# Cached attention on one core: V loaded head by head in K's key order, P normalized in blocks of 64

## The chip, the cores and the metric

The kernel runs on one core of one Trainium2 chip. The metric is the device time of one execution in microseconds (us). Before the change three runs gave 849.04, 850.43 and 854.05 us, median 850.43 us. The profile is of one further execution.

## The reference

Two independent blocks, A and B, of the same shapes are computed and laid side by side in the output. Each is attention over a cache, in bf16:

```python
B, Sq, D = 16, 64, 640            # batches, queries, model width
H, Sk, Dh = 32, 512, 128          # heads, cached keys, head width
q = (x @ wq).reshape(B, Sq, H, Dh).transpose(0, 2, 1, 3)
scores = einsum("bhqd,bhkd->bhqk", q, k_cache) * Dh ** -0.5
p = softmax(scores, axis=-1)
o = einsum("bhqk,bhkd->bhqd", p, v_cache)
out = o.transpose(0, 2, 1, 3).reshape(B, Sq, H * Dh) @ wo
```

Each of the four caches (K and V of A and B) has 16 x 32 x 512 x 128 elements of 2 bytes, 67.1 MB. They make up nearly all the 292 MB that the core reads.

## The kernel before

**Tiling.** The work is cut into 512 steps: a step is one head of two batches (a "batch pair"), 2 x 64 query rows on 128 partitions. Two steps are a macro-step, 256 in all; two macro-steps (four heads, G = 4) are a chunk. A pass is half of the heads (16) of one block over its 8 batch pairs; there are four passes.

**One macro-step m.** K of two heads and two batches comes by one load (LDK, L792, 512 KB) into the ring kn_ring. Partition p of a head holds the 8 consecutive keys 8p to 8p+7. TensorE transposes it in 32 pieces (KX, L586), so that column 64 t + p of the transposed K is key 8p + t; DVE copies that from PSUM to SBUF (KE, L593). Then per step: the scores (SM, L632), the negated row maximum on DVE (MX, L641), the exponential with row sum on ACT (EX, L647), the reciprocal on DVE (RC2, L653) and the normalization P times reciprocal on POOL (NM, L661), which writes pn_ring. TensorE transposes the normalized P in four pieces of 128 columns per step (TR2, L670); the transposed P is copied out of PSUM (TE on DVE, L680, or TA on ACT, L684), and TensorE multiplies it with V (PV2, L694). The results of a chunk leave PSUM on ACT (OE4, L701) and are multiplied with WO (OP2, L709, and OX, L719). The projection of Q (L603) and the transposes of x (L804, L813) run in between.

**Order of keys between P and V.** P's columns come in K's order, 64 t + p. V is loaded so that partition r holds the 4 consecutive keys 4r to 4r+3. NM closes the gap: it writes its columns in another order, so that piece tl of 128 columns has at place r the key 4r + tl:

```python
src = p_ring[:, g % NP, :].rearrange("q (th tl pp) -> q th tl pp", th=2, tl=4)
dst = pn_ring[:, g % NPN, :].rearrange("q (tl pp th) -> q th tl pp", tl=4, th=2)
```

Neighbours of the source land two elements apart in the destination.

**V.** One load per chunk and batch (LDV, L789, 512 KB, 256 in all) brings four heads of one batch into v_ring, which has 5 chunk slots (NVP). Each partition gets 4 x 1 KB. A slot is free for the load five chunks later once the second PV2 of its chunk has run.

**What sets the order.** Nothing is decided at run time. The order on TensorE, ACT, DVE and POOL comes from the templates PHASES: lists of (operation, offset in macro-steps, sub-index, due time in a period of 6.3 us), repeated for every chunk. Loads are sorted by a planned time and all issued on SP's queue, those of K, V, WQ, WO and x in one line; only the stores of the output are issued by ACT. The planner keeps a running time, which advances by DMA_US for each load (1.40 us for LDK, 1.44 for LDV), and makes each load wait for the TensorE operation that is planned just before it, at the latest BEFORE = 3.88 macro-steps ahead of its first use. LEAD and WLEAD are how far ahead loads are aimed for, STEP_US and START_US the planner's idea of TensorE's pace. Waits between engines are semaphores; a V slot has one semaphore of its own.

Of the kernel before, what the change touches and what calls it, by code (L numbers as in the profile page):

```python
# [15 lines left out]
class Cfg:  # L16
    G = 4
# [5 lines left out]
    LEAD = 5.37  # L23
    WLEAD = 5.48
    STEP_US = ((8, 3.68), (32, 27.17), (160, 3.12), (216, 3.1), (256, 3.43))
    DMA_US = dict(LDK=1.40, LDV=1.44, LDWQ=1.8, LDWO=1.8, LDX=0.45, LDXR=0.5)
    START_US = 210.96
    BEFORE = 3.88
# [17 lines left out]
         (("OE4", -4, 0, 0.38), ("QEZ", 0, 0, 0.43), ("QEZ", 0, 1, 1.68), ("OVP", -1, 0, 2.62), ("QEZ", 0, 2, 2.72),  # L46
          ("EX", 1, 0, 2.78), ("QEZ", 0, 3, 3.12), ("QEZ", 0, 4, 3.5), ("EX", 1, 1, 3.54), ("QEZ", 0, 5, 3.88),
          ("EX", 0, 1, 4.51), ("OXP", -13, 0, 4.63), ("QEJ", 4, 0, 4.64), ("TA2", -2, 0, 4.76), ("EX", 0, 0, 5.06),
          ("QEZ", 0, 7, 5.11), ("QEN", -6, 0, 5.12), ("QEZ", 0, 6, 5.49), ("ST", -45, 0, 6.19)),
         (("KE", 4, 0, 0.07), ("XIE", 2, 1, 0.91), ("MX", 0, 0, 0.95), ("MX", 0, 1, 0.96), ("RC2", -1, 0, 0.99),  # L50
          ("MX", 1, 0, 1.46), ("OXF", 47, 0, 2.01), ("MX", 1, 1, 2.78), ("OVF", -23, 0, 3.45), ("TE2", -1, 0, 3.61),
          ("XIE", 2, 2, 3.73), ("XIE", 2, 3, 3.96), ("KE", 3, 0, 4.55), ("XIE", 6, 0, 4.58), ("XIE", 0, 4, 4.84),
          ("XIE", -4, 6, 4.98), ("XIE", -2, 5, 5.43), ("RC2", 0, 0, 5.63), ("XIE", 0, 7, 6.21)),
# [6 lines left out]
         (("OE4", -4, 0, 0.38), ("QEZ", 0, 0, 1.23), ("OXP", -13, 0, 1.5), ("EX", 0, 1, 1.52), ("OVP", -17, 0, 1.59),  # L60
          ("EX", 0, 0, 1.89), ("XTE", 28, 0, 2.28), ("QEZ", 0, 1, 2.45), ("QEN", -6, 0, 2.53), ("ST", -35, 0, 3.16),
# [22 lines left out]
          ("QEN", -6, 0, 3.07), ("TA2", -2, 0, 3.72), ("OXP", -3, 0, 4.37), ("OVP", -3, 0, 4.78), ("EX", 1, 1, 5.06),  # L84
          ("XTE", 0, 0, 5.27)),
         (("KE", 3, 0, 0.07), ("RC2", -1, 0, 0.53), ("MX", 0, 0, 1.15), ("MX", 0, 1, 1.7), ("MX", 1, 0, 1.78),
          ("KE", 2, 0, 2.61), ("MX", 1, 1, 3.18), ("RC2", 0, 0, 3.78), ("OXF", -3, 0, 4.23), ("TE2", -1, 0, 4.74),
          ("OVF", -3, 0, 5.58)),
# [9 lines left out]
          ("OXF", -3, 0, 6.18)),  # L98
# [12 lines left out]
    )  # L111
    TRB = (2, 3)
    OXB = 4
    OXH = False
    KTB = (6, 6)
    NWU = 32

# [22 lines left out]
def build_plan(dims, cfg):  # L140
# [73 lines left out]
    def bank(i):  # L214
        return ("PB", i)
# [173 lines left out]
    def sem_key(op):  # L389
        if op.kind in ("LDK", "LDV", "LDXR"):  # L390
            return ("d_" + op.kind[2:].lower(), op.writes[0][1])
# [542 lines left out]
```

## Time and profile before

| what | value |
|---|---|
| median of three runs | 850.43 us (849.04 to 854.05) |
| profiled execution, time | 852.97 us |
| profiled execution, span from first to last instruction | 851.0 us |
| granted TensorE clock, mean | 0.998 |
| TensorE busy | 811.3 us (95%) |
| DVE busy | 727.9 us (86%) |
| ACT busy | 644.7 us (76%) |
| POOL busy | 417.1 us (49%) |
| read from HBM | 292.03 MB, 346 GB/s over the span with the 2.62 MB written |
| one V load (512 KB), issue to landing, median | 6.8 us in block A, 6.5 us in block B |
| one K load (512 KB), issue to landing, median | 6.5 us in block A, 6.3 us in block B |
| one normalization on POOL (L661) | 843 ns, 512 of them |

Busy times are summed over instructions of one engine, so shares of different engines overlap. "Issue to landing" runs from the DMA's issue on its queue to its completion. A packet in the profile's DMA rows is one contiguous piece that one DMA engine moves, or the small write with which an engine reports that its part of a transfer is complete. There are 16 DMA engines; "share of 16 engines" is the sum of all packets' times over 16 spans.

### The profile page before, as it was taken

Reading aid. Unit: us, or ns where it says so; the run is one execution under the profiler, and the core shown is the slowest. Engines: PE = TensorE matmul, PEld = TensorE weight load, DVE = VectorE, ACT = ScalarE, POOL = GpSimd, SP = SyncE. Lnnn points to the kernel's source line nnn. Section 1 sums busy time; section 2 is a strip of 40 time slices with the busy share of each in tenths; the row PEclk is TensorE's granted clock in tenths of the full one; section 3 lists DMA queues with packets and bytes.
Section 4 is the critical chain, followed back from the end, with each engine's and each line's share of the span. In section 5 each row is a group of like instructions: output and inputs, shape, how many; then the busy total and the mean of one; then the engine's idle time right before and its main releaser. Section 6 shows DMA issues by size and latency. Waiting matters only on the chain.

```text
span 851.0 us, 38366 instructions
## 1 busy us (share of the span) xinstructions
PE 811.3 (95%) x17025; PEld 566.4 (67%) x17156; DVE 727.9 (86%) x1192; ACT 644.7 (76%) x1466; POOL 417.1 (49%) x518
## 2 busy tenths in 40 slices
PE   8999999999999999999999998999999999999996
PEld 5566676666666666666666666666666666666664
DVE  4688888888888898888899887988888989989994
ACT  2678877777777787777877877787887877778886
POOL 0355455454544554454554545455455455455553
PEclk9999999999999999999999999999999999999999
DMA  9999999999999999999999999999999999999992
GB/s 306 360 354 349 369 354 352 348 338 362 354 352 353 369 369 363 359 360 367 364 362 367 364 360 349 321 362 362 360 360 363 366 369 365 366 339 352 370 321 89
DMA packets 228438, 297.14 MB, mean 349 GB/s; under 512 B 9136, under 2 KB 162736, under 8 KB 228272
## 3 DMA queue, kind: packets, MB, share of 16 engines
q1 hardware_dynamic: 225968, 292.06, 100.3%
q8 instruction: 134, 2.20, 1.1%
q10 hardware_dynamic: 2304, 2.62, 0.9%
q14 instruction: 32, 0.26, 0.1%
HBM read 292.03 MB, written 2.62 MB: 346 GB/s over the span
## 4 chain that ended last, share of the span: by engine, by line
PE 89%; issue 3%; ACT 3%; DMA 2%; DVE 2%; SPq 0%; ACTq 0%
PE ps L586 17%; PE ps L694 15%; PE ps L603 15%; PE ps L632 14%; PE ps L670 13%; PE ps L709 12%; PE ps L719 3%; ACT p_ring L647 2%; DMA v_ring<-in_A_v_cache_dram 1%; DVE negmax L641 1%; ACT pT_ring L684 1%; DMA wq_sb<-in_A_wq_dram 1%; DVE ktp_ring L593 1%; PE ps L804 0%; PE ps L813 0%
## 5 line engine op out<-in xcount | busy, mean ns | idle before, releaser
L661 POOL TENSOR_SCALAR pn_ring<-p_ring,recip 128x512 bf16<-128x512 bf16 x512 | 416.4, 843 | 425.1 <-DVE recip L653 379.0
L647 ACT ACTIVATE p_ring<-ps,negmax 128x512 bf16<-128x512 f32 x512 | 349.0, 688 | 74.0 <-DVE negmax L641 68.5
L593 DVE COPY ktp_ring<-ps 128x2048 bf16<-128x2048 bf16 x256 | 312.1, 1219 | 56.3 <-PE ps L586 56.2
L641 DVE TENSOR_REDUCE negmax<-ps 128x1 f32<-128x512 f32 x512 | 328.3, 683 | 16.2 <-PE ps L632 8.5
L586 PEld LDWEIGHTS ps<-ident,kn_ring 64*128 64x128 bf16 x8192 | 136.8, 95 | 107.9 <-issue 96.4
L586 PE MATMUL ps<-ident,kn_ring 64*128 64x64 bf16 x8192 | 169.2, 191 | 3.3 <-issue 1.4
L603 PE MATMUL ps<-xT_sb,wq_sb 128*128 128x512 bf16 (+2 forms) x543 | 133.4, 372 | 19.0 <-issue 18.1
L670 PEld LDWEIGHTS ps<-ident,pn_ring 128*128 128x128 bf16 x2048 | 125.4, 98 | 38.8 <-ACT p_ring L647 7.2
L694 PE MATMUL ps<-pT_ring,v_ring 128*128 128x64 bf16 x4096 | 143.5, 194 | 2.8 <-issue 1.9
L701 ACT ACTIVATE oT_ring<-ps 128x512 bf16<-128x512 f32 x128 | 76.4, 597 | 91.7 <-PE ps L694 91.7
L684 ACT ACTIVATE pT_ring<-ps 128x1024 bf16<-128x1024 bf16 (+1 forms) x144 | 140.9, 987 | 3.0 <-DVE pT_ring L680 2.2
L670 PE MATMUL ps<-ident,pn_ring 128*128 128x128 bf16 x2048 | 138.9, 219 | 3.4 <-issue 1.6
L709 PE MATMUL ps<-wo_sb,oT_ring 128*128 128x512 bf16 x498 | 135.3, 379 | 4.0 <-issue 1.9
L632 PE MATMUL ps<-ktp_ring,qc_ring 128*64 128x512 bf16 x1024 | 135.5, 385 | 0.7 <-issue 0.7
L694 PEld LDWEIGHTS ps<-pT_ring,v_ring 128*128 128x128 bf16 x4096 | 128.2, 98 | 9.6 <-issue 2.4
L647 ACT ACTIVATION_READ_ACCUMULATOR p_ring<-ps,negmax 128x1 f32 x512 | 104.8, 205 | 0.0
L680 DVE COPY pT_ring<-ps 128x1024 bf16<-128x1024 bf16 (+1 forms) x128 | 82.5, 644 | 14.6 <-PE ps L670 14.1
L619 ACT ACTIVATE qc_ring<-ps 128x512 bf16<-128x512 f32 (+1 forms) x129 | 76.8, 596 | 21.5 <-PE ps L603 21.4
L603 PEld LDWEIGHTS ps<-xT_sb,wq_sb 128*128 128x128 bf16 x660 | 53.8, 98 | 54.0 <-issue 1.1
L632 PEld LDWEIGHTS ps<-ktp_ring,qc_ring 128*64 128x64 bf16 x1024 | 47.2, 109 | 34.1 <-issue 1.3
L709 PEld LDWEIGHTS ps<-wo_sb,oT_ring 128*128 128x128 bf16 x512 | 42.7, 98 | 25.0 <-ACT pT_ring L684 2.1
L653 DVE RECIPROCAL recip<-rowsum 128x2 f32<-128x2 f32 x256 | 39.8, 155 | 4.4 <-ACT p_ring L647 4.4
(21 smaller groups left out, 127.2 us busy)
## 6 DMA issues: line engine op xcount, KB each, us to landing
kn_ring<-in_A_k_cache_dram SPq DMA_DIRECT2D x128, 512.0 KB, 6.5
v_ring<-in_A_v_cache_dram SPq DMA_DIRECT2D x128, 512.0 KB, 6.8
kn_ring<-in_B_k_cache_dram SPq DMA_DIRECT2D x128, 512.0 KB, 6.3
v_ring<-in_B_v_cache_dram SPq DMA_DIRECT2D x128, 512.0 KB, 6.5
wq_sb<-in_A_wq_dram SPq DMA_DIRECT2D x8, 640.0 KB, 7.1
wo_sb<-in_A_wo_dram SPq DMA_DIRECT2D x8, 640.0 KB, 7.2
wq_sb<-in_B_wq_dram SPq DMA_DIRECT2D x8, 640.0 KB, 6.8
wo_sb<-in_B_wo_dram SPq DMA_DIRECT2D x8, 640.0 KB, 6.6
```

The source lines that it names most:

```text
L586: last = e.transpose(kt_ps[hs][:, 64 * t:64 * t + 64], kn_ring[r, m % NKB, t // 8, t % 8 * DH:(t % 8 + 1) * DH], ident[r, r])
L593: ins = e.tensor_copy(ktp_ring[:, ktslot(op.idx)], ps[:, b:b + 2, :].rearrange("p b s -> p (b s)").bitcast(BF16))
L603: last = e.matmul(dst[:, col:col + n], wq_sb[:, qslot(hh // G), kt, (hh % G) * DH:(hh % G + 1) * DH], xT_sb[:, kt, lo * 128:hi * 128], sta ...
L632: ins = e.matmul(s_bank(g)[64 * j:64 * j + 64, :], q[:, 64 * j:64 * j + 64], kt[:, sub, j], start=True, stop=True, tile_position=(0, 64 * j))
L641: ins = e.reduce_max(negmax[:, r:r + 1], s_bank(g), axis=AX.X, negate=True)
L647: ins = e.activation(p_ring[:, g % NP, :], s_bank(g), ACTF.Exp, bias=negmax[:, r:r + 1], scale=1.0, accum_out=rowsum[:, r:r + 1])
L661: ins = e.tensor_scalar(dst, src, recip[:, r:r + 1], 1.0, ALU.mult, ALU.mult)
L670: ins = e.transpose(pt_flat(m)[:, (4 * sub + t) * 128:(4 * sub + t + 1) * 128], pn_ring[:, g % NPN, t * 128:(t + 1) * 128], ident[:, :])
L680: ins = e.tensor_copy(*pt_copy(op.idx, op.aux))
L684: ins = e.activation(*pt_copy(op.idx, op.aux), ACTF.Copy)
L694: ins = e.matmul(qo_ps[:, col:col + 64], v_ring[:, m // 2 % NVP, j, 2 * (m % 2) + sub, t * DH:(t + 1) * DH], pT_ring[:, m % NT, sub, t, 64 ...
L709: ins = e.matmul(out_ps, oT_ring[:, m // 2 % NO, 2 * (m % 2) + sub, :], wo_sb[:, wslot(ps_, hh // G), hh % G, 0:N0], start=(hh == 0), stop ...
```

## The change

V is loaded by one transfer per head and batch (128 KB, 1,024 in all) instead of one per four heads and batch. Within a head, partition th x 64 + p now holds the four keys 8p + 4 th to 8p + 4 th + 3, which is the numbering of K's rows. NM therefore leaves the 64 elements that belong to one (th, tl) together and only exchanges the order of these blocks. A PV2 waits for the four V transfers of its own two heads (one semaphore for each half of a V slot), and the slot's halves are freed and reloaded one by one. The planner's numbers and the templates PHASES are others: the kinds of operation in them are the same, at other due times and with some other offsets. The numbers of instructions of TensorE, ACT and DVE are unchanged.

```diff
-    LEAD = 5.37
-    WLEAD = 5.48
-    STEP_US = ((8, 3.68), (32, 27.17), (160, 3.12), (216, 3.1), (256, 3.43))
-    DMA_US = dict(LDK=1.40, LDV=1.44, LDWQ=1.8, LDWO=1.8, LDX=0.45, LDXR=0.5)
-    START_US = 210.96
-    BEFORE = 3.88
+    LEAD = 5.29
+    WLEAD = 5.77
+    STEP_US = ((8, 2.69), (32, 25.43), (160, 3.11), (216, 3.06), (256, 2.73))
+    DMA_US = dict(LDK=1.40, LDV=0.36, LDWQ=1.8, LDWO=1.8, LDX=0.45, LDXR=0.5)
+    START_US = 154.11
+    BEFORE = 3.97
...
     PHASES = (
...
         (112,
-         (("SM", 0, 0, 0.0), ("SM", 0, 1, 0.21), ("SM", 1, 0, 0.43), ("SM", 1, 1, 0.64), ("KX", 2, 0, 0.79),
-          ("OP2", -4, 0, 2.67), ("TR2", -2, 0, 2.98), ("OP2", -3, 0, 3.28), ("TR2", -1, 0, 3.46),
-          ("OX", -3, 0, 4.35), ("KX", 5, 0, 4.38), ("PV2", -2, 0, 5.77), ("PV2", -1, 0, 6.05)),
+         (("SM", 0, 0, 0.0), ("SM", 0, 1, 0.21), ("SM", 1, 0, 0.43), ("SM", 1, 1, 0.64), ("KX", 2, 0, 1.97),
+          ("OP2", -4, 0, 2.31), ("OP2", -3, 0, 3.17), ("TR2", -2, 0, 3.25), ("TR2", -1, 0, 3.28),
+          ("OX", -3, 0, 3.62), ("KX", 5, 0, 4.24), ("PV2", -2, 0, 4.74), ("PV2", -1, 0, 5.05)),
...
         if kind == "PV2":
-            return mk("pe", "PV2", m, [("pT", m % cfg.NT, 0), ("pT", m % cfg.NT, 1), ("v", k % cfg.NVP, 0), ("v", k % cfg.NVP, 1)], [bank(1)], ts)
+            return mk("pe", "PV2", m, [("pT", m % cfg.NT, i) for i in range(2)] + [("v", k % cfg.NVP, j, i) for j in range(2) for i in (g0 % G, g1 % G)], [bank(1)], ts)
...
-        add([("PV2", 2 * (k - cfg.NVP) + 1, 0)] if k >= cfg.NVP else [], ("PV2", 2 * k, 0), cfg.LEAD - j, 2, "LDV", m,
-            [("v", k % cfg.NVP, j)], m)
+        for i in range(G):
+            add([("PV2", 2 * (k - cfg.NVP) + i // 2, 0)] if k >= cfg.NVP else [], ("PV2", 2 * k + i // 2, 0), cfg.LEAD - j + i // 2, 2, "LDV", m,
+                [("v", k % cfg.NVP, j, i)], (m, i))
...
     def sem_key(op):
-        if op.kind in ("LDK", "LDV", "LDXR"):
+        if op.kind == "LDV":
+            return ("d_v", op.writes[0][1], op.aux[1] // 2)
+        if op.kind in ("LDK", "LDXR"):
             return ("d_" + op.kind[2:].lower(), op.writes[0][1])
...
         def em_NM(e, op):
-            src = p_ring[:, g % NP, :].rearrange("q (th tl pp) -> q th tl pp", th=2, tl=4)
-            dst = pn_ring[:, g % NPN, :].rearrange("q (tl pp th) -> q th tl pp", tl=4, th=2)
+            src = p_ring[:, g % NP, :].rearrange("q (th tl p) -> q th tl p", th=2, tl=4)
+            dst = pn_ring[:, g % NPN, :].rearrange("q (tl th p) -> q th tl p", tl=4, th=2)
...
-            if op.kind == "LDV":
-                h0 -= h0 % G
-                src = blocks[blk][2][2 * bp + m % 2, h0:h0 + G].rearrange("g (p t) d -> p g (t d)", p=128)
-                ins = e.dma_start(v_ring[:, m // 2 % NVP, m % 2], src)
...
+        def em_LDV(e, op):
+            m, i = op.aux
+            blk, bp, grp, ps_, hh0 = step_info(2 * m)
+            h = (ps_ % NHALF) * HH + hh0 - hh0 % G + i
+            src = blocks[blk][2][2 * bp + m % 2, h].rearrange("(p th t) d -> th p (t d)", th=2, t=4)
+            ins = e.dma_start(v_ring[:, m // 2 % NVP, m % 2, i], src)
+            return ins, ins
```

More of the change, by code (lines that the diff above doesn't have):

```diff
@@ L39 @@
         (0,
[6 rows of a table removed]
[L46 to L53, printed above, removed]
[6 rows of a table removed]
-         (("OE4", -4, 0, 0.38), ("QEZ", 0, 0, 1.23), ("OXP", -13, 0, 1.5), ("EX", 0, 1, 1.52), ("OVP", -17, 0, 1.59),
-          ("EX", 0, 0, 1.89), ("XTE", 28, 0, 2.28), ("QEZ", 0, 1, 2.45), ("QEN", -6, 0, 2.53), ("ST", -35, 0, 3.16),
[22 rows of a table removed]
[L84 to L88, printed above, removed]
[9 rows of a table removed]
-          ("OXF", -3, 0, 6.18)),
[12 rows of a table removed]
[6 rows of a table added]
@@ new lines @@
+         (("OVP", -15, 0, 0.19), ("OE4", -4, 0, 0.33), ("QEZ", 0, 0, 0.65), ("EX", 1, 0, 0.8), ("QEJ", 4, 0, 0.89),
+          ("QEZ", 0, 1, 1.6), ("QEZ", 0, 2, 2.06), ("OXP", -7, 0, 2.92), ("QEZ", 0, 3, 2.97), ("QEN", -6, 0, 3.31),
[4 rows of a table added]
+          ("OVF", -21, 0, 4.26), ("KE", 3, 0, 4.83), ("TE2", -1, 0, 4.83), ("XIE", 2, 2, 5.0), ("XIE", -2, 5, 5.21),
+          ("RC2", 0, 0, 5.23), ("XIE", -4, 6, 5.99), ("XIE", 2, 3, 6.01), ("XIE", 0, 7, 6.05)),
[7 rows of a table added]
+          ("EX", 0, 0, 2.38), ("QEZ", 0, 1, 3.21), ("QEN", -6, 0, 3.44), ("EX", 1, 0, 3.54), ("QEZ", 0, 2, 3.65),
+          ("TA2", -2, 0, 4.23), ("XTE", 30, 0, 4.73), ("QEZ", 0, 3, 4.84), ("OVP", -11, 0, 5.73), ("EX", 1, 1, 6.07)),
[10 rows of a table added]
+          ("XTE", -12, 0, 5.73)),
[10 rows of a table added]
+          ("OXP", -3, 0, 6.18)),
+         (("KE", 3, 0, 0.32), ("RC2", -1, 0, 0.52), ("MX", 0, 0, 1.32), ("MX", 0, 1, 1.76), ("MX", 1, 0, 1.8),
+          ("KE", 2, 0, 3.1), ("RC2", 0, 0, 4.68), ("TE2", -1, 0, 4.99), ("MX", 1, 1, 5.12), ("OVF", -3, 0, 5.13),
+          ("OXF", -3, 0, 5.79)),
[9 rows of a table added]
+          ("OVF", -3, 0, 5.7)),
[11 rows of a table added]
@@ L780, in em_LDX, with em_LDK @@
             return ins, ins
-        def em_LDKV(e, op):
+        def em_LDK(e, op):
             m = op.aux
@@ L785, in em_LDKV @@
             h0 = (ps_ % NHALF) * HH + hh0
-            if op.kind == "LDV":
-                h0 -= h0 % G
-                src = blocks[blk][2][2 * bp + m % 2, h0:h0 + G].rearrange("g (p t) d -> p g (t d)", p=128)
-                ins = e.dma_start(v_ring[:, m // 2 % NVP, m % 2], src)
-            else:
-                src = blocks[blk][1][2 * bp:2 * bp + 2, h0:h0 + 2].rearrange("j hs (p t) d -> (hs p) j (t d)", t=8)
-                ins = e.dma_start(kn_ring[:, m % NKB], src)
+            src = blocks[blk][1][2 * bp:2 * bp + 2, h0:h0 + 2].rearrange("j hs (p t) d -> (hs p) j (t d)", t=8)
+            ins = e.dma_start(kn_ring[:, m % NKB], src)
+            return ins, ins
[5 more added lines that the diff above has]
+            ins = e.dma_start(v_ring[:, m // 2 % NVP, m % 2, i], src)
             return ins, ins
@@ L839, in mha_kernel @@
                         OVP=em_OVP, OXP=em_OXP, OVF=em_OVF, OXF=em_OXF, ST=em_ST, INIT1=em_INIT1, INIT2=em_INIT2,
-                        LDWQ=em_LDWQ, LDWO=em_LDWO, LDX=em_LDX, LDXR=em_LDXR, XT=em_XT, XTE=em_XTE, XI=em_XI, XIE=em_XIE, WU=em_WU, LDK=em_LDKV, LDV=em_LDKV)
+                        LDWQ=em_LDWQ, LDWO=em_LDWO, LDX=em_LDX, LDXR=em_LDXR, XT=em_XT, XTE=em_XTE, XI=em_XI, XIE=em_XIE, WU=em_WU, LDK=em_LDK, LDV=em_LDV)
         def full(s, v):
```

96 rows, old and new, of the table PHASES are left out of this document.

## The prediction, made before the changed kernel ran

> **What bounds the kernel now.** I read the page's DMA parts first, because loads are what the change rewrites, then the waits of TensorE and of the SP queue, then the view of the V tile. Engines, DMA load and packets, from the page:
>
> ```profile
> PE 811.3 (95%) x17025; PEld 566.4 (67%) x17156; DVE 727.9 (86%) x1192; ACT 644.7 (76%) x1466; POOL 417.1 (49%) x518
> ...
> DMA  9999999999999999999999999999999999999992
> GB/s 306 360 354 349 369 354 352 348 338 362 354 352 353 369 369 363 359 360 367 364 362 367 364 360 349 321 362 362 360 360 363 366 369 365 366 339 352 370 321 89
> DMA packets 228438, 297.14 MB, mean 349 GB/s; under 512 B 9136, under 2 KB 162736, under 8 KB 228272
> ...
> q1 hardware_dynamic: 225968, 292.06, 100.3%
> q10 hardware_dynamic: 2304, 2.62, 0.9%
> ```
>
> TensorE is busy 95% of the span and the 16 DMA engines are busy in every slice but the last: two limits lie on top of each other. Of TensorE's own waits, the loads cause hardly any, while the SP queue, which issues every load, waits for TensorE again and again (columns: us in total, times, longest):
>
> ```profile
> PE ps L586 <- DMA v_ring<-in_A_v_cache_dram: 0.7, 1, 0.7
> ```
>
> ```profile
> SPq L792 <- PE ps L632: 103.6, 74, 2.9
> SPq L792 <- PE ps L709: 78.5, 73, 2.6
> ```
>
> So the loads arrive in time and are paced by TensorE, with little to spare: a load path that is somewhat slower has no idle engine to take it up. The V tile's view gives issue cost (min/median/max ns) and flight time:
>
> ```profile
> L789 SPq DMA_DIRECT2D v_ring<-in_A_v_cache_dram x128: 367/368/3549, 15.8 to 432.6; - x128
> L789 SPq DMA_DIRECT2D v_ring<-in_B_v_cache_dram x128: 367/368/1122, 436.3 to 834.9; - x128
> DMA to landing us min/median/max: 3.7/6.7/11.7
> ```
>
> Two more readings I need. First, the price of a packet on its DMA engine. In the trace's packet records 1,024-byte packets most often take 46 ns (mean 49.4), 2,048-byte ones 84 ns (mean 91.2), 1,280-byte ones 55 ns, and 4-byte completion packets 9 ns. Pricing all packets at these usual values fills 16 engines to 0.998 at most in any 21 us stretch and to 0.974 in the median one, so the usual values are one engine's service times, one packet after the other, and not overlapped latencies. Second, over how many engines a transfer is cut. There are 555 loads and 16 stores, 571 transfers; 571 x 16 = 9,136, exactly the packets under 512 B. So each transfer ends with one completion packet on every one of 16 engines. All 571 have access patterns that open with a count of 128 on both the HBM and the SBUF side.
>
> **The V load: how many engines.** Before, V's source is p g (t d): 128 x 4 x 512 elements. After, it is th p (t d): 2 x 64 x 512. The two outer counts can't be fused into 128, since th steps 1 KB and p steps 2 KB; the destination is still 128 partitions of one row. No transfer of before opens with anything but 128, so the number of engines a V load will use is not shown. The bounds are 16 (all 571 rows) and 2, if a transfer is dealt out along the outermost count of both sides: 2 and 128 have only 2 and 1 as common divisors. I take 2. The nearest rows agree with dealing along the outermost count and don't show any dealing inside it; the partition count alone, which stays 128, would give 16 and is the case against me.
>
> [...]
>
> **The sum with two engines, the same two each time.** V is 2 blocks x 16 x 32 x 512 x 128 x 2 bytes = 134.2 MB, 131,072 packets of 1 KB, unchanged in size and number. On two engines that is 65,536 each. Engine-time on either of them:
> - V: 65,536 x 46 ns = 3,015 us.
> - K stays on 16: 65,536 / 16 = 4,096 x 84 ns = 344 us.
> - WQ 10,240 / 16 x 46 ns = 29 us; WO and x 10,240 / 16 x 55 ns = 35 us; stores 7 us; completions (1,024 + 315) x 9 ns = 12 us; instruction fetch (1.1% of 851) 9 us.
> Together 3,451 us. Nothing hides it: per macro-step (one of 256) the two engines need 4 heads x 64 x 46 ns + 16 x 84 ns = 13.1 us, where TensorE's share now is 811.3 / 256 = 3.2 us. Loads are issued some four macro-steps ahead (BEFORE), some 50 us of work for the two engines, so they don't run dry, and K loads, which share the ring of those two engines, finish only behind V packets. V begins 16 us into the span and the last V load is issued 16 us before its end; about 13 us of the K, WQ and x work runs before V starts, and the end after the last V landing is 10 us: +13 us. Span about 3,465 us. The usual price of 46 ns is met by 66% of V-size packets while all 16 engines compete; with HBM traffic down to a quarter, I allow 0.4% over it: span 3,478, and the profiled execution's time stands 2.0 us above its span (852.97 against 851.0), so 3,480 us. The median of the runs is 850.43, 2.5 below the profiled one, which is nothing at this size.
>
> Bounds: at the shortest packets of the records (44 and 81 ns) V is 2,884 and K 332 us, the sum 3,308 and the time about 3,320. At the mean prices under today's contention (49.4 and 91.2 ns, others as above) V is 3,237, K 374, the sum 3,703 and the time about 3,720. A check from the page alone: 292.06 MB in 100.3% of 16 x 851 us is 21.4 GB/s per engine; 67.1 MB of V and 9.9 MB of the rest at that rate take 3,600 us, and at the best slice (370 / 16 = 23.1 GB/s) 3,330 us.
>
> **The other parts.** *Issues.* V goes from 256 to 1,024 transfers on SP's queue: +768. The nearest row is 0.367 us per issue whatever the size; for the unequal patterns take 0.367 to 1 us. A macro-step then has five issues, 1.8 to 5 us, hidden under 13.1 us; behind each V issue stand the K, WQ, WO and x loads of the same queue, and they are late only by what the two engines already impose. If the transfers kept 16 engines, that cover is gone: 1,323 SP issues x 0.367 = 486 us of 851, and the queue becomes the limit at 851 / 1,323 = 0.64 us each. *Completions.* With 16 engines 768 x 16 = 12,288 more packets, x 9 ns / 16 = 6.9 us; with two, fewer than now. *P in blocks of 64.* POOL's 512 normalizations (L661) take 843 ns for 512 elements with the written elements two apart; afterwards they run through blocks of 64. Not shown; bounds 0 gain to 843 ns gained, and on the other side double. POOL is busy 49%, 3.4 us (four of them) of a 6.3 us period of two macro-steps, so even double its time fits in a period of 26 us: nothing. *Ring freed by halves.* Each V load now waits only for the PV2 that reads its half chunk, up to one macro-step (3.2 us) earlier. With two engines the ring isn't short, nothing. *Order and pace.* The templates for TensorE, ACT, DVE and POOL are permuted and SP's planned times shifted; the instruction counts of TensorE, ACT and DVE are the same. TensorE is unoccupied for 851.0 - 811.3 = 39.7 us now, so the permutation is worth between -40 and, taken alike, +40 us where TensorE is the limit, and nothing where it waits for V.
>
> **The rivals.** *Sixteen engines after all, slower by completions (chance 0.06).* The partition count decides, or the pattern is re-cut. The engines are 97.4% filled by the usual prices, so 6.9 us more of packets go almost wholly to the end, 858 us (with the permutation unknown, 845 to 890). For it: the SBUF side is 128 as ever. Against it: the source can't be cut in 16 along its outermost count.
> *Sixteen engines, faster (0.04).* Finer V loads and earlier-freed halves even out the 0.974 filling: the 2.6% missing is 22 us, less 6.9 us for completions, so 837 us. It decides if completion packets lie in gaps rather than between data packets. Against it: the SP queue waits for TensorE and not for V slots.
> *Sixteen engines, SP the limit (0.01).* At 1 us an issue, 1,323 us. Against: every load row, 160 to 640 KB, has a median of 0.34 to 0.53 us.
> *Two engines, but another pair each time (0.02).* One V load then lasts 64 x 46 ns = 2.9 us instead of 1.5, inside the 6.7 us flight and the lead of four macro-steps; total engine work is unchanged, so about 851 us.
>
> **How the numbers follow.** Two engines, always the same: 0.87, because all 571 transfers are dealt out evenly where both sides open with 128 and nothing in the trace suggests that a count further in can be dealt out instead; time 3,480 us, own range 3,320 to 3,720. The range is this case's own, since the others together hold 0.13 and leaving them out is within 2 in 10. A measurement of this kernel tells apart about 0.5%. Faster by more than that: 0.04, the second rival. Within 0.5%: 0.03, the rotating pair and a part of the first rival. Slower: 0.87 + 0.05 + 0.01 = 0.93.
>
> **What would show it.** Right: packets under 512 B at 299 x 16 + 16 x 16 + 1,024 x 2 = 7,088 (with 16 engines 21,424); GB/s near 85 in all slices; the DMA row at 2 or 3 tenths with q1 near 25% of 16 engines; TensorE at some 23% and waiting above all for V; V's flight time in tens of us, because transfers queue on two engines. POOL's 512 normalizations near 0.8 us, whatever they are, would not matter. Wrong: 21,424 small packets and a time near 850; or 7,088 small packets with the DMA row still at 9 and a time near 850, which would mean that the pairs rotate; or two engines at a packet price clearly away from 46 ns, which would shift the time in proportion of 3,015 us.

## The result and the profile after

The changed kernel takes 3,268.61 us (median of 4 runs, 3,268.25 to 3,269.02) against 849.73 us (848.61 to 854.05) for the kernel before beside it: a ratio of 3.843, 95% interval 3.829 to 3.857. The direction and the mechanism are those of the prediction; the time is 6% under its 3,480 us and below its range, which began at 3,320.

The same rows of the page as for the kernel before, now of the changed kernel:

```profile
span 3266.9 us, 39264 instructions
...
PE 1126.0 (34%) x17156; PEld 737.7 (23%) x17156; DVE 740.0 (23%) x1192; ACT 667.6 (20%) x1466; POOL 349.7 (11%) x518
...
DMA  5222222222232222222222222222223222222221
GB/s 160 97 82 87 83 93 83 94 89 95 96 100 89 86 91 90 96 86 93 97 98 96 88 86 83 95 89 87 89 90 100 98 87 85 84 84 93 84 84 51
DMA packets 226396, 297.18 MB, mean 91 GB/s; under 512 B 7088, under 2 KB 160688, under 8 KB 226224
...
q1 hardware_dynamic: 223920, 292.06, 26.9%
```

The bytes and the number of V packets are the same, the mean fill of the 16 DMA engines fell from 9 tenths to 2, and the packets under 512 B are 7,088: 299 x 16 + 16 x 16 + 1,024 x 2. Each V load has left two completion packets, so each ran on two engines. A mean of 2 tenths does not mean that the DMA side has room: two engines of sixteen that never rest, and fourteen that carry only their part of K, give such a mean. The packet records bear this out. Packets of V's size start from 15.0 to 3,258.1 us of the span, and between 16 and 3,258 us two or more packets are in flight for all but 11 us, exactly two for 2,065 us. Pairs of engines that changed from load to load would have more V packets in flight at once. The records carry no engine's number, so they don't say which two.

What TensorE waits for (us in total, times, longest):

```profile
PE ps L695 <- DMA v_ring<-in_A_v_cache_dram: 1039.0, 62, 19.4
...
PE ps L695 <- DMA v_ring<-in_B_v_cache_dram: 1001.0, 64, 22.1
```

2,040 us of waiting stand ahead of PV2 (L695), in 126 waits for 128 chunks. The chain that ended last, by engine and by line, shows a trap:

```profile
SPq 58%; DMA 27%; PE 13%; issue 1%; DVE 0%; ACT 0%
SPq L797 44%; DMA v_ring<-in_A_v_cache_dram 14%; SPq L788 13%; DMA v_ring<-in_B_v_cache_dram 12%; PE ps L695 4%; PE ps L633 3%; PE ps L604 2%; PE ps L587 2%; PE ps L710 1%; PE ps L671 1%; DMA kn_ring<-in_A_k_cache_dram 1%; SPq L774 1%; DMA kn_ring<-in_B_k_cache_dram 0%; SPq L766 0%; SPq L802 0%
```

```profile
L797 SPq DMA_DIRECT2D v_ring<-in_A_v_cache_dram x512: 538/2808/4332, 15.1 to 1640.7; - x171
L797 SPq DMA_DIRECT2D v_ring<-in_B_v_cache_dram x512: 583/2658/4019, 1643.6 to 3248.0; - x171
```

The chain puts most on SP's queue, and a V issue lasts 2.7 us in the median. 1,024 of these would fill 2,800 us, so "SP has become the limit" reads as well from this page as "two engines are the limit". The minimum of 0.54 us speaks for back-pressure: SP can issue a V load in 0.54 us, and by my reading the issue is held up while the two engines still have work in line; no record shows how much they have. So do the issues of K, whose pattern did not change, with a median of 0.37 us before (L792) and 2.59 us after (L788):

```profile
L792 SPq DMA_DIRECT2D kn_ring<-in_A_k_cache_dram x128: 367/368/3161, 0.8 to 411.1; - x128
```

```profile
L788 SPq DMA_DIRECT2D kn_ring<-in_A_k_cache_dram x128: 368/2592/3357, 1.7 to 1560.3; - x128
```

The experiments decide it.

### The profile page after: what moved, and what is told of

Its sections match the earlier page's. It is cut to its first block, busy times and chain, and to the rows that moved or that the text cites. A ratio compares the mean times of both kernels' runs of the same rounds, so it can differ in the third digit from the quotient of the medians.

```text
span 3266.9 us, 39264 instructions
## 1 busy us (share of the span) xinstructions
PE 1126.0 (34%) x17156; PEld 737.7 (23%) x17156; DVE 740.0 (23%) x1192; ACT 667.6 (20%) x1466; POOL 349.7 (11%) x518
## 2 busy tenths in 40 slices
DMA packets 226396, 297.18 MB, mean 91 GB/s; under 512 B 7088, under 2 KB 160688, under 8 KB 226224
## 3 DMA queue, kind: packets, MB, share of 16 engines
q1 hardware_dynamic: 223920, 292.06, 26.9%
## 4 chain that ended last, share of the span: by engine, by line
SPq 58%; DMA 27%; PE 13%; issue 1%; DVE 0%; ACT 0%
SPq L797 44%; DMA v_ring<-in_A_v_cache_dram 14%; SPq L788 13%; DMA v_ring<-in_B_v_cache_dram 12%; PE ps L695 4%; PE ps L633 3%; PE ps L604 2%; PE ps L587 2%; PE ps L710 1%; PE ps L671 1%; DMA kn_ring<-in_A_k_cache_dram 1%; SPq L774 1%; DMA kn_ring<-in_B_k_cache_dram 0%; SPq L766 0%; SPq L802 0%
## 5 line engine op out<-in xcount | busy, mean ns | idle before, releaser
L695 PE MATMUL ps<-pT_ring,v_ring 128*128 128x64 bf16 x4096 | 242.4, 241 | 2040.0 <-DMA v_ring<-in_A_v_cache_dram 1039.0
L695 PEld LDWEIGHTS ps<-pT_ring,v_ring 128*128 128x128 bf16 x4096 | 222.1, 130 | 2055.5 <-DMA v_ring<-in_A_v_cache_dram 1046.3
L662 POOL TENSOR_SCALAR pn_ring<-p_ring,recip 128x512 bf16<-128x512 bf16 x512 | 349.0, 695 | 2873.7 <-PE ps L671 2314.6
L633 PE MATMUL ps<-ktp_ring,qc_ring 128*64 128x512 bf16 x1024 | 246.6, 619 | 46.9 <-DMA kn_ring<-in_B_k_cache_dram 46.9
L587 PE MATMUL ps<-ident,kn_ring 64*128 64x64 bf16 x8192 | 198.5, 206 | 13.1 <-DMA v_ring<-in_A_v_cache_dram 9.4
L587 PEld LDWEIGHTS ps<-ident,kn_ring 64*128 64x128 bf16 x8192 | 164.9, 105 | 137.2 <-issue 118.6
L710 PE MATMUL ps<-wo_sb,oT_ring 128*128 128x512 bf16 x512 | 180.6, 438 | 7.4 <-DMA kn_ring<-in_B_k_cache_dram 5.0
L604 PE MATMUL ps<-xT_sb,wq_sb 128*128 128x512 bf16 (+2 forms) x660 | 166.1, 387 | 0.4 <-ACT qc_ring L620 0.2
L671 PEld LDWEIGHTS ps<-ident,pn_ring 128*128 128x128 bf16 x2048 | 136.1, 102 | 43.5 <-issue 6.9
L633 PEld LDWEIGHTS ps<-ktp_ring,qc_ring 128*64 128x64 bf16 x1024 | 70.3, 157 | 132.7 <-issue 62.7
L604 PEld LDWEIGHTS ps<-xT_sb,wq_sb 128*128 128x128 bf16 x660 | 66.5, 105 | 87.5 <-issue 28.6
```

The costliest lines, as they stand in the source:

```text
L587: last = e.transpose(kt_ps[hs][:, 64 * t:64 * t + 64], kn_ring[r, m % NKB, t // 8, t % 8 * DH:(t % 8 + 1) * DH], ident[r, r])
L604: last = e.matmul(dst[:, col:col + n], wq_sb[:, qslot(hh // G), kt, (hh % G) * DH:(hh % G + 1) * DH], xT_sb[:, kt, lo * 128:hi * 128], sta ...
L633: ins = e.matmul(s_bank(g)[64 * j:64 * j + 64, :], q[:, 64 * j:64 * j + 64], kt[:, sub, j], start=True, stop=True, tile_position=(0, 64 * j))
L662: ins = e.tensor_scalar(dst, src, recip[:, r:r + 1], 1.0, ALU.mult, ALU.mult)
L671: ins = e.transpose(pt_flat(m)[:, (4 * sub + t) * 128:(4 * sub + t + 1) * 128], pn_ring[:, g % NPN, t * 128:(t + 1) * 128], ident[:, :])
L695: ins = e.matmul(qo_ps[:, col:col + 64], v_ring[:, m // 2 % NVP, j, 2 * (m % 2) + sub, t * DH:(t + 1) * DH], pT_ring[:, m % NT, sub, t, 64 ...
```

## The experiments

Theory A goes on from the completions so far (16 engines for 128 and 128, 2 for 2 and 128): a load runs on as many engines as the largest common divisor of the outer counts of its two patterns, up to the 16 that there are, and equal loads on the same ones. Its price comes from the changed kernel's packet records: where only V packets run, an engine starts a new one every 42 or 43 ns (381 ns for nine in a row; 42.35 ns in the mean), although each record lasts 46 ns. With two engines at work, the next start but one is the next on the same engine: in stretches of V-size packets alone it comes 42 or 43 ns later in 96,999 of 108,050 cases, and 46 ns later in 86. 2 KB packets start about every 80.3 ns (80 in unbroken rows) and last 84. The load of one of the two engines is then 65,536 x 42.35 ns = 2,775 us of V and 417 us of K and the rest, 3,192 us of the span of 3,267; 75 us are left for the ends and for contention. Rival B: SP's issues are the limit. Rival C: the price is the full 46 ns, as predicted, and something else saved time.

**Other outer counts.** Four variants of the changed kernel: V's source opens with 4, 8 or 16 (v_outer4, v_outer8, v_outer16), or the key order is undone with 128 rows and the old normalization (v_rows128).

```diff
v_outer4 (u=8 and u=16 in the other two):
-            src = blocks[blk][2][2 * bp + m % 2, h].rearrange("(p th t) d -> th p (t d)", th=2, t=4)
+            src = blocks[blk][2][2 * bp + m % 2, h].rearrange("(p u t) d -> u p (t d)", u=4, t=4)
v_rows128:
-            src = p_ring[:, g % NP, :].rearrange("q (th tl p) -> q th tl p", th=2, tl=4)
-            dst = pn_ring[:, g % NPN, :].rearrange("q (tl th p) -> q th tl p", tl=4, th=2)
+            src = p_ring[:, g % NP, :].rearrange("q (th tl pp) -> q th tl pp", th=2, tl=4)
+            dst = pn_ring[:, g % NPN, :].rearrange("q (tl pp th) -> q th tl pp", tl=4, th=2)
...
-            src = blocks[blk][2][2 * bp + m % 2, h].rearrange("(p th t) d -> th p (t d)", th=2, t=4)
+            src = blocks[blk][2][2 * bp + m % 2, h].rearrange("(p t) d -> p (t d)", t=4)
```

> V's source opens with 4 x 32 instead of 2 x 64 (partition u x 32 + p holds keys 16p + 4u to 16p + 4u + 3), all else as in the changed kernel; P is not reordered to fit, so V's rows stand beside other keys' P, with the same work. [...] Theory B (SP's issues of an unequal pattern are the limit, 2.6 us each as the changed kernel's row has them): 1,024 such issues as in the changed kernel, so 3,270 us again. Theory C (the packet price is the full 46 ns and something else saved time in the changed kernel): the step from 2 to 4 engines saves 1,507 us, so 1,760 us.

> V's source opens with 8 x 16, all else as in the changed kernel; P is not reordered to fit, with the same work. Theory A: an engine's load is 16,384 x 42.35 ns = 694 us of V and 417 us of the rest, 1,111 us, with ends and contention 1,130 to 1,210 us; 299 x 16 + 256 + 1,024 x 8 = 13,232 packets under 512 B. Theory B (SP issues): 3,270 us. Theory C (46 ns): 2 to 8 engines saves 2,261 us, 1,007 us.

> V's source opens with 16 x 8, so its outer count still differs from the destination's 128; all else as in the changed kernel; P is not reordered to fit, with the same work. Theory A: the largest common divisor is 16, the load of an engine is 347 + 417 = 764 us, less than TensorE's 811, so the time falls back to the kernel before: 840 to 890 us, with 299 x 16 + 256 + 1,024 x 16 = 21,424 packets under 512 B. Theory A' (only a pattern that opens with 128 on both sides is spread over all engines): well over 1,000 us. Theory B (SP issues, 2.6 us for an unequal pattern): 3,270 us; by the shortest issue of the changed kernel, 0.538 us, 1,024 x 0.54 + 299 x 0.37 = 661 us on SP, which does not limit. POOL's normalization: 695 ns if the blocks of 64 make it short, 843 ns if it was short only because the other engines idled.

> The key order is undone: V's source is 128 rows of 1 KB again and P is normalized in the old interleaved order; per-head loads, halves of a slot, planner numbers and templates stay those of the changed kernel. Theory A: 16 engines, 840 to 890 us; what is left against the kernel before is the price of per-head loads (6.9 us of completions if the engines' queues were the limit) and of the other order. Theory B: SP's issue at 0.37 us, 486 us on SP: 850 us too, so B is told apart by v_outer16 and not here. POOL's normalization: 843 ns.

Measured: 1,938.0 us with 4 and 1,361.6 us with 8 (one run each), 1,151.8 us with 16 (1.353 times before, interval 1.348 to 1.357), 854.5 us with 128 rows (1.0044, 1.0012 to 1.0077). The packet rows of the first three, in this order, one page each:

```profile
DMA packets 228444, 297.19 MB, mean 154 GB/s; under 512 B 9136, under 2 KB 162736, under 8 KB 228272
```

```profile
DMA packets 232540, 297.21 MB, mean 219 GB/s; under 512 B 13232, under 2 KB 166832, under 8 KB 232368
```

```profile
DMA  9999999999999999999999999999999999999994
...
DMA packets 240732, 297.24 MB, mean 258 GB/s; under 512 B 21424, under 2 KB 175024, under 8 KB 240560
...
q1 hardware_dynamic: 238256, 292.11, 103.1%
```

The completion packets are 9,136, 13,232 and 21,424 to the unit, which is 299 x 16 + 256 and 1,024 x 4, x 8 and x 16: 4, 8 and 16 engines per V load, as A has it. With 4, the records again have four or more packets in flight for all but 9 us from 16 us on to the last V packet. Rival B falls: the number of issues is the same in all of these and the time goes from 3,269 to 1,152 us. The median V issue goes from 2.7 us over 1.3 and 0.9 to 0.60 us at 16 engines:

```profile
L797 SPq DMA_DIRECT2D v_ring<-in_A_v_cache_dram x512: 536/600/4382, 14.7 to 586.8; - x171
```

The 2.7 us are about what the two engines need for one V load, 64 x 42.35 ns = 2.71 us. Rival C, which forecast 1,760 and 1,007 us with 4 and 8, falls too.

But the times miss A's as well, the more the more engines there are: 1,938 against A's sum for 4, 32,768 x 42.35 ns = 1,388 us of V and 417 us of the rest, 1,805 in all before ends and contention, 1,362 against 1,111, with ends and contention at most 1,210, and 1,152 against at most 890. The time with 16 fits A', but its reason does not: all 16 engines took part. With 16 engines A forecast TensorE as the limit again, and the DMA engines are full instead, at 258 GB/s. The packet records became longer: those of V's size last 47.2 ns in the mean on two engines, 49.7 on 4, 55.4 on 8 and 69.1 on 16, against 48.8 in v_rows128, where 16 engines move the same bytes. So a second thing depends on the outer count.

**What makes packets long.** Theory P: the side toward SBUF does it, where engines that are dealt runs of neighbouring partitions would collide; this is a guess, and no record names an engine or a partition. Theory H: the 16 KB steps of v_outer16 in HBM are slow. v_blocks8 keeps the 16 x 8 pattern and makes the HBM pieces contiguous; v_stride4k keeps 128 rows and spreads them in HBM; v_halves opens with 64 on both sides.

```diff
v_blocks8 and v_stride4k, from the changed kernel (the two last lines are one each):
-            h = (ps_ % NHALF) * HH + hh0 - hh0 % G + i
-            src = blocks[blk][2][2 * bp + m % 2, h].rearrange("(p th t) d -> th p (t d)", th=2, t=4)
+            h0 = (ps_ % NHALF) * HH + hh0 - hh0 % G
+            src = blocks[blk][2][2 * bp + m % 2, h0:h0 + G].rearrange("h k d -> (h k) d").rearrange("(u i p t) d -> i u p (t d)", i=4, p=8, t=4)[i]
+            src = blocks[blk][2][2 * bp + m % 2, h0:h0 + G].rearrange("h k d -> (h k) d").rearrange("(p i t) d -> i p (t d)", i=4, t=4)[i]
v_halves, from the kernel before, for th in (0, 1), with the changed kernel's normalization and LDV=0.72:
...
-                src = blocks[blk][2][2 * bp + m % 2, h0:h0 + G].rearrange("g (p t) d -> p g (t d)", p=128)
-                ins = e.dma_start(v_ring[:, m // 2 % NVP, m % 2], src)
+                src = blocks[blk][2][2 * bp + m % 2, h0:h0 + G].rearrange("g (p th t) d -> th p g (t d)", th=2, t=4)[th]
+                ins = e.dma_start(v_ring[64 * th:64 * th + 64, m // 2 % NVP, m % 2], src)
```

> Like v_outer16, V's source opens with 16 x 8 against 128 partitions, but the 8 rows of one outer index now lie together in HBM (8 KB in one piece, pieces 32 KB apart) where v_outer16 steps 16 KB between them; the four loads of a chunk and batch divide its 512 KB among themselves, so V's rows stand beside other heads' and keys' P, with the same work. Theory P (a load that is dealt out in runs of neighbouring partitions makes its engines collide on the SBUF side): packets as long as in v_outer16 (mean 69 ns), 1,120 to 1,180 us. Theory H (v_outer16 was slow because its engines step through HBM in 16 KB strides): packets near 49 ns again, 845 to 890 us.

> V's source opens with 128 as before, but its rows of 1 KB are 4 KB apart; per-head loads, P in blocks of 64, planner and templates as in the changed kernel; V's rows stand beside other heads' and keys' P, with the same work. Theory P: all 16 engines in the usual dealing, 845 to 870 us. Theory H: long packets, over 950 us. POOL under full load: 692 to 695 ns if the blocks make the normalization short, about 841 ns if the idling of others did.

> The kernel before with the change's key order, P in blocks of 64, and each V load split in two: 64 partitions by 4 heads, 256 KB, source and destination both open with 64, so that 16 engines take part; 512 V loads. Planner numbers of before, LDV 0.72. The result is the reference's. Theory A alone: 16 engines, 845 to 870 us. [...] POOL: 692 to 695 ns.

Measured: v_blocks8 1,160.3 us (1.359, 1.350 to 1.368), v_stride4k 856.6 us (1.0074, 1.0053 to 1.0095), v_halves between 1,248.7 and 1,282.9 us in four runs, above the 870 us of A and above what P allowed: even V packets at twice 42.35 ns, 8,192 x 84.7 = 694 us on an engine, make only 1,111 us with 417 us of the rest. Its profile is of one of 1,274.2 us. V-size packets last 70.1, 48.8 and 78.7 ns in the mean. Of v_blocks8's, v_stride4k's and v_halves' pages, in this order:

```profile
DMA packets 240732, 297.24 MB, mean 256 GB/s; under 512 B 21424, under 2 KB 175024, under 8 KB 240560
```

```profile
DMA  8989999999999999999999999999999999999993
...
DMA packets 240732, 297.24 MB, mean 349 GB/s; under 512 B 21424, under 2 KB 175024, under 8 KB 240560
```

```profile
DMA packets 232536, 297.18 MB, mean 234 GB/s; under 512 B 13232, under 2 KB 166832, under 8 KB 232368
```

The completions say 16 engines per V load in all three (for v_halves, 299 x 16 + 256 + 512 x 16 = 13,232). H falls twice: contiguous HBM pieces didn't help, and 4 KB steps didn't hurt. Of the two theories P is left: with 128 rows on both sides 16 engines keep 349 GB/s, with 16 x 8 toward the same 128 partitions they get 256 to 258, and with loads of 64 partitions 234, at 78.7 ns a packet against 48.8 in v_stride4k. Why these packets are long was not shown: that engines collide on the side toward SBUF remains my guess, and it doesn't give the time of v_halves.

v_halves keeps the change's key order on 16 engines, and at 1,249 us or more it is no way out: it trades two engines for sixteen whose V packets last 78.7 ns in the mean.

**The price of a packet.**

Both come from the changed kernel, with LDV=0.72. half_of_v loads and uses every second head of V; two_engines_2kb makes one load for two heads.

```diff
half_of_v:
...
-        for i in range(G):
+        for i in range(0, G, 2):
...
-                        ins = e.matmul(qo_ps[:, col:col + 64], v_ring[:, m // 2 % NVP, j, 2 * (m % 2) + sub, t * DH:(t + 1) * DH],
+                        ins = e.matmul(qo_ps[:, col:col + 64], v_ring[:, m // 2 % NVP, j, 2 * (m % 2), t * DH:(t + 1) * DH],
two_engines_2kb:
...
-            src = blocks[blk][2][2 * bp + m % 2, h].rearrange("(p th t) d -> th p (t d)", th=2, t=4)
+            src = blocks[blk][2][2 * bp + m % 2, h:h + 2].rearrange("h k d -> (h k) d").rearrange("(p th t) d -> th p (t d)", th=2, t=8)
-            ins = e.dma_start(v_ring[:, m // 2 % NVP, m % 2, i], src)
+            ins = e.dma_start(v_ring[:, m // 2 % NVP, m % 2, i:i + 2].rearrange("q g e -> q (g e)"), src)
```

> The changed kernel with V in packets of 2 KB: one load for two heads, the source opens with 2 x 64 rows of 2 KB, so still two engines; 512 V loads instead of 1,024; V's rows stand beside other keys' P, with the same work. Theory A with the start-to-start prices of the changed kernel's records (42.35 ns for 1 KB, 80.3 ns for 2 KB): V is 32,768 x 80.3 = 2,631 us on an engine instead of 2,775, 4.6 us less of completions: 3,269 - 149 = 3,120 us, 3,060 to 3,150. With the prediction's prices (46 and 84 ns, one after the other) V is 2,753 us, the whole 3,220 us. If SP's issues were the limit: 512 of 1,024 V issues gone, about 2,000 us.

> The changed kernel with every second V load left out: only heads 0 and 2 of a chunk are loaded, and TensorE uses each of them for two heads, the same multiplications on half of V. 512 V loads, still 2 x 64 rows of 1 KB on two engines. Theory A (a V packet costs 42.35 ns start to start and 1.15 ns of contention, 43.5 ns): 32,768 x 43.5 = 1,425 us and 5 us of completions fewer, 3,269 - 1,430 = 1,839 us, 1,800 to 1,870. Theory C (46 ns one after the other, and contention on top): 32,768 x 47.15 = 1,545 us and 5 us fewer, 1,719 us, up to 1,760.

two_engines_2kb took 3,173.4 us (one run), halfway between the 3,120 of A and the 3,220 of the predicted prices and outside A's 3,060 to 3,150, so its time decides nothing between them; it does speak once more against B, which expected some 2,000. Its records do decide the spacing: with 65,536 V packets of 2 KB, the next start but one comes 80 ns later 43,500 times, 82 or 83 ns later 9,499 times, and 84 ns later 322 times. Why the whole is longer than A's sum stays open. half_of_v took 1,877.4 us (one run), 3,268.6 - 1,877.4 = 1,391.2 us less. That is above C's 1,760 at most and just above A's 1,870 at most. Less 5 us of completions, that is 1,386 us for 32,768 packets: 42.3 ns each, the start-to-start price and not 46. A's own 43.5 was too much: the 75 us beyond the engines' work did not shrink with V (span 1,875.5 against 1,388 + 412 = 1,800 us), so contention isn't a surcharge per V packet. K, which is the same in both, may carry it; no run tests that.

**What 16 engines would have cost.** planner_only is the kernel before with the changed kernel's planner numbers and templates alone (LDV stays 1.44). per_head_only is the kernel before with per-head V loads and halves of a V slot alone (LDV=0.36):

```diff
per_head_only:
...
-            src = blocks[blk][2][2 * bp + m % 2, h0:h0 + G].rearrange("g (p t) d -> p g (t d)", p=128)
-                ins = e.dma_start(v_ring[:, m // 2 % NVP, m % 2], src)
...
+            src = blocks[blk][2][2 * bp + m % 2, h].rearrange("(p t) d -> p (t d)", t=4)
+            ins = e.dma_start(v_ring[:, m // 2 % NVP, m % 2, i], src)
```

> The kernel before with the changed kernel's templates and planner numbers alone (LDV stays 1.44); V loads and normalization of before. If the 0.4 to 0.7% that the 16-engine versions v_rows128 and v_stride4k lose come from the other order and pace: 854 to 857 us. If they come from the 768 more transfers: 850 us.

> The kernel before with per-head V loads alone (128 rows of 1 KB, 1,024 loads, halves of a slot, LDV 0.36); templates, planner numbers, key order and normalization of before. If the loss comes from the 12,288 more completion packets: 12,288 x 9 ns / 16 = 6.9 us at most, 853 to 858 us. If it comes from order and pace: 850 us. If finer loads even out the engines' filling: under 846 us.

planner_only 857.0 us, ratio 1.0057 (1.0031 to 1.0083); per_head_only 854.2 us, 1.0039 (1.0012 to 1.0066). Both are slightly slower than before, and their intervals overlap, so which of the two weighs more stays open. Per-head loads cost 3.3 us (1 to 6) of 852, less than the 6.9 us that the completions would cost if the engines were full.

## Why the prediction was right and where it was wrong

**Two engines, the same two.** Right. The count (7,088) and the series over 2, 4, 8 and 16 show two engines for a load; the packets in flight, two for most of the span, and the time itself show that it is the same two for every load. The trace of before shows neither term, the two or the same two: they were my choice, and the 3,480 us were added up on it. The changed kernel then showed 1,024 x 2 completions and exactly two packets in flight for 2,065 us; which two of the sixteen engines they are, no record says.

**The price of a V packet: the term that was mis-sized.** The step that failed reads: "so the usual values are one engine's service times, one packet after the other, and not overlapped latencies". I had inferred that from a fill of at most 0.998 at 46 and 84 ns in the kernel before. That is too near 1 to carry it: redone on the same records the highest fill of a 21 us stretch is 0.99 to 1.01, by where the stretches begin and whether instruction fetches count, and at the true spacing it would have been 0.94. Records of neighbouring packets on one engine overlap by 3 to 4 ns; in stretches of V packets alone an engine starts one every 42.35 ns. The V term is 65,536 x 42.35 = 2,775 us where I had 3,015, K is 329 where I had 344, the smaller rows together 88 where I had 92. That takes 259 us off. My allowances for the ends (13) and for contention (14) became 75 us, 48 more: 3,480 - 259 + 48 = 3,269 us. The 75 us are what is left over and not a measured cost; as V's packets start from 15 to 3,258 us, most of them lie inside that stretch, where the two engines hardly rest. The lower bound failed for the same reason: 44 ns is the shortest duration of a record, which bounds the spacing of starts only if records don't overlap. The test of the premise was at hand in the old trace, where a start-to-start spacing was never read. Of its 65,536 packets of 2 KB, 35,249 have another such start exactly 80 ns later, and 7,937 one exactly 84 ns later, no more than at the lags beside it. For its V-size packets, too, the peak stands at 42 and 43 ns and there is none at 46.

**What bounded the kernel before.** "With little to spare" was too strong on the DMA side. At 42.35 and 80.3 ns the packets of before fill the engines to about 757 of 851 us, 89%. This is an estimate, without what 16 engines at once do to each other. By it TensorE, busy 95%, is the nearer limit, which fits per_head_only, where 12,288 more completion packets cost 3.3 us and not 6.9.

**Issues.** The bounds of 0.367 to 1 us held: 0.536 us at least and 0.60 us in the median for an unequal pattern with 16 engines (v_outer16), 0.43 us for equal ones (v_rows128). The 2.7 us of the changed kernel are not the price of an issue, as K's issues (0.37 us before, 2.59 us after) and the series over 2, 4, 8 and 16 engines (2.7, 1.3, 0.9 and 0.60 us) show; that they are back-pressure is my reading of it.

**P in blocks of 64.** "Nothing" was right for the time. POOL itself did get faster, which I had left open. The normalization before, in the changed kernel, and in v_stride4k under full load:

```profile
L661 POOL TENSOR_SCALAR pn_ring<-p_ring,recip 128x512 bf16<-128x512 bf16 x512 | 416.4, 843 | 425.1 <-DVE recip L653 379.0 <-PE ps L670 46.2
```

```profile
L662 POOL TENSOR_SCALAR pn_ring<-p_ring,recip 128x512 bf16<-128x512 bf16 x512 | 349.0, 695 | 2873.7 <-PE ps L671 2314.6
```

```profile
L662 POOL TENSOR_SCALAR pn_ring<-p_ring,recip 128x512 bf16<-128x512 bf16 x512 | 348.1, 693 | 494.8 <-DVE recip L654 294.1
```

843 ns became 693 to 695 ns, also where DVE and DMA are as busy as before, and 841 ns in v_rows128 with the old order: it is the access pattern, and not the idling of the others. Before, POOL had 425 us to spare, so nobody waited for these 77 us.

**Order and pace.** Between -40 and +40 us was allowed; alone they cost 0.57% of 852, 4.8 us.

**The rivals.** Sixteen engines with 128 rows on both sides give 854 to 857 us (v_rows128, v_stride4k) where I had 858 for the slower rival; the faster one, 837, is not seen in any run with 16 engines. None of my rivals had 16 engines with longer packets, as in v_outer16's 1,152 us (69.1 ns against 48.8 in v_rows128): the number of engines alone does not settle the price of a load.

**What would show it.** GB/s is 91 where I said 85, q1 26.9% for 25%, as the shorter time gives. TensorE is 34% busy and not 23%: its granted clock was 0.638 in the changed kernel (0.998 before), and a PV2 matmul took 241 ns where it had taken 194. With 2,040 us of waiting for V that should have cost nothing, though no run tests it. V's flight time in tens of us can't be read, since the page has no landing times for V. K loads, which go through the same two engines, landed after 9.6 to 9.7 us in the median, where they had taken 6.3 to 6.5, so the loads seem to have waited at SP's issue more than in flight.

## What to carry to other kernels

Before changing the layout of a load, look at the outermost counts of both patterns as they are issued: here counts of 2, 4, 8 and 16 against 128 put a V load on 2, 4, 8 and 16 DMA engines, and the number of completion packets (7,088 to 21,424) showed it. When a mean DMA share drops and the time rises (9 tenths to 2, 850 to 3,269 us), ask whether a few engines carry everything, and compare the median of a DMA issue with its minimum (2.7 and 0.54 us) before taking it for the price of an issue. To price packets on one engine, measure from start to start, since recorded durations may overlap (46 ns every 42.35 ns here).

## What the runs showed of the hardware that I had not expected

- In stretches of V packets alone an engine of the changed kernel starts a 1 KB packet every 42.35 ns although its record lasts 46 ns: 24.2 GB/s for one engine, confirmed by 42.3 ns from half_of_v.
- Sixteen engines are not enough: with an outer count of 16 toward 128 partitions they moved 256 to 258 GB/s, with 128 on both sides 349, whichever of the tried steps the HBM side had (v_outer16, v_blocks8, v_stride4k).
- Loads of 64 partitions on 16 engines are slower still: 234 GB/s, packets of 78.7 ns in the mean, 1,249 to 1,283 us (v_halves).
- POOL's multiplication of 512 bf16 elements takes 843 ns when it writes every second element and 693 to 695 ns when it writes runs of 64.
